# Moving a softmax product and a weight cast of the first batch to GpSimd, and giving its first kv group a bank of its own

## The chip, the cores and the metric

The kernel runs on one core of one Trainium2 chip. The metric is the device time of one execution in microseconds (us); each comparison alternates both kernels on the same chip. A trace covers the span from the first to the last instruction, which is some 1.8 us shorter than the time.

## The reference

Eight batches of attention with separate softmaxes on q and k, then a two-layer network with a swish.

```python
q_s = softmax(q, over head_dim)            # q, k, v: (8, 8, 576, 64), fp32
k_s = softmax(k, over the sequence)
kv  = einsum('bhsd,bhse->bhde', k_s, v)
x   = einsum('bhsd,bhde->bhse', q_s, kv)   # regrouped to (4608, 512)
h   = x @ w_in                             # 512 x 2048
out = (h * sigmoid(beta * h)) @ w_out      # 2048 x 512
```

## The kernel before

The schedule is written by hand: each engine executes its instructions in the order of the program. Batch 0 alone starts with nothing in the chip, so its loads, exponentials, transposes, kv products and weight casts stand in a row. "Pair" is two of the eight heads; `V`, `A`, `G` are VectorE, ScalarE, GpSimd. The helpers that the change touches:

```python
def q_mul(b, s, n=2, eng=nc.vector):       # divides the exponentials by their sums; two SBUF inputs
    eng.tensor_tensor(eq[b][:, :, h, :], eq[b][:, :, h, :],
                      rq[b][:, 1, :, h].unsqueeze(3).to_broadcast((P, R, m, D)), ALU.mult)
def tpe(b, j, tag): ...                    # TensorE transposes pair j into the bank `tag`
def q_ev(b, j, eng): ...                   # copies that bank to SBUF
def vz_cast(b, j, eng, ...): ...           # casts v to bf16 for the kv group j
def kvz_mm(b, j, tag, n): ...              # TensorE: kv of pair j; kvz_norm divides it on VectorE
def xpe(c, j, tag): ...                    # TensorE: x of pair j; xev evicts it
def w_castk(blk, kt, eng): ...             # casts one 128x512 slice of w_in
def hpe(c, j, kts, tag): ...               # TensorE: h[j] += w_in slices kts @ x
def warm(n, tag): ...                      # n dummy matmuls that keep TensorE busy
```

The head of batch 0 (cut; `...` marks cuts):

```python
    q_sum(0, 1, 4)
    q_mul(0, 2, 4)
    kz_exp(0, 0)
    q_mul(0, 1, 4)
    ...
    tpe(0, 3, "acc1")
    tpe(0, 2, "acc3")
    ...
    q_ev(0, 2, V)
    vz_cast(0, 0, G)
    tpe(0, 1, "acc2")
    kvz_mm(0, 0, "acc3", 1)      # waits for the eviction of pair 2 from acc3
    ...
    q_ev(0, 1, V); q_ev(0, 3, V)
    ...
    hpe(0, 2, [3]); hpe(0, 4, [0], "b3") ...   # h of batch 0; blocks j = 4..7 need w_in block 1
```

The softmax here doesn't subtract the row's maximum and nothing guards it: scores larger than these inputs give would overflow.

Of the kernel before, what the change touches and what calls it, by code (L numbers as in the profile page):

```python
# [17 lines left out]
def kernel(  # L18
# [151 lines left out]
    def evac(eng, dst, src):  # L170
        if eng is nc.scalar:
            eng.copy(dst, src)  # L172
        else:
            eng.tensor_copy(dst, src)  # L174
# [8 lines left out]
    def kz_exp(b, j):  # L183
        if j == 0:
            ek_buf(b)
        nc.scalar.activation(ek[b][:, j, :], k_st[b][:, j, :], ACTF.Exp)  # L186
# [28 lines left out]
    def vz_cast(b, j, eng, m=1, part=None):  # L215
        r = slice(0, RW) if part is None else (slice(0, 5), slice(5, RW))[part]
        evac(
            eng,
            va[b][:, j : j + m, r, 0:D],
            v_st[b][:, j : j + m, :].rearrange("p j (i d) -> p j i d", i=RW)[:, :, r, :],  # L220
        )
# [35 lines left out]
    def q_sum(b, s, n=2):  # L257
        if s == 0:
            rq[b] = work.tile([P, 2, R, H], F32, tag="rq", bufs=2, name=f"rq{b}")
        m = H // n  # L260
        h = slice(s * m, (s + 1) * m)
        nc.vector.tensor_reduce(rq[b][:, 0, :, h], eq[b][:, :, h, :], axis=AX.X, op=ALU.add)  # L262
        nc.vector.reciprocal(rq[b][:, 1, :, h], rq[b][:, 0, :, h])  # L263

    def q_mul(b, s, n=2, eng=nc.vector):
        m = H // n
        h = slice(s * m, (s + 1) * m)
        eng.tensor_tensor(  # L268
            eq[b][:, :, h, :],
            eq[b][:, :, h, :],  # L270
            rq[b][:, 1, :, h].unsqueeze(3).to_broadcast((P, R, m, D)),
            ALU.mult,
        )
# [11 lines left out]
    def bank(tag):  # L285
        if tag not in turns:
            return tag
        turns[tag] += 1
        return (HB if tag == "h" else AB)[(turns[tag] - 1) % 2]
# [3 lines left out]
    def tpe(b, j, tag):  # L293
        if j == 0:
            qsT[b] = work.tile([P, R, HP, P], BF16, tag="qsT", bufs=2, name=f"qsT{b}")
        tp_of[b, j] = ps.tile([P, R, P], BF16, tag=bank(tag), bufs=1, name=f"tp{b}_{j}")
        for i in range(R):
            nc.tensor.transpose(  # L298
                tp_of[b, j][:, i, :],
                eq[b][:].rearrange("p i (j x) d -> p i j (x d)", j=HP)[:, i, j, :],  # L300
                identity[:],
            )

    def q_ev(b, j, eng):
        evac(eng, qsT[b][:, :, j, :], tp_of.pop((b, j))[:])

    def kvz_mm(b, j, tag=None, n=1):
        if tag is not None:
            t = ps.tile([P, n, D1], F32, tag=bank(tag), bufs=1, name=f"kv{b}_{j}")
            for jl in range(n):  # L310
                att_of[b, j + jl] = t[:, jl : jl + 1, :]
            att_of[b, j, n] = t
        t = att_of[b, j]
        for i in range(RW):
            for e in range(2):
                r = slice(e * D, (e + 1) * D)
                nc.tensor.matmul(  # L317
                    t[r, 0, :],
                    ek[b][r, j, ds(i * D, D)],
                    va[b][r, j, i, :],  # L320
                    start=(i == 0),
                    stop=(i == RW - 1),
                    tile_position=(e * D, e * D),
                )
# [62 lines left out]
    def xpe(c, j, tag):  # L387
        t = x_ps[c, j] = ps.tile([P, MAIN], F32, tag=bank(tag), bufs=1, name=f"x{c}_{j}")
        nc.tensor.matmul(t[:], kvp[:, c, j, :], qsT[c][:, :, j, :])  # L389

    def xev(c, j, eng, part=None):
        n = MAIN // 2
        cols = slice(0, MAIN) if part is None else slice(part * n, part * n + n)
        evac(eng, x_of(c)[:, j, cols], x_ps[c, j][:, cols])
# [4 lines left out]
    def hpe(c, j, kts, tag="h"):  # L399
        if (c, j) not in h_of:  # L400
            h_of[c, j] = ps.tile([P, MAIN], F32, tag=bank(tag), bufs=1, name=f"h{c}_{j}")
        h = h_of[c, j]
        for kt in kts:
            nc.tensor.matmul(  # L404
                h[:],
                w_unit(j, kt),
                x_of(c)[:, kt, :],
                start=(kt == 0),
                stop=(kt == KT - 1),
            )  # L410
# [117 lines left out]
    def warm(n, tag):  # L528
        t = ps.tile([P, 512], F32, tag=bank(tag), bufs=1, name=f"warm{warm_n[0]}")
        warm_n[0] += 1  # L530
        for _ in range(n):
            nc.tensor.matmul(t[:], xT[2][:, 0, 0:P], xT[2][:, 0, :])  # L532

    V, A, G = nc.vector, nc.scalar, nc.gpsimd
# [22 lines left out]
    def w_castk(blk, kt, eng):  # L557
        evac(eng, w_in_b[blk][kt][:, 0, :], wst["in", blk][:, kt, :])
# [3 lines left out]
    def beta_pe(tag):  # L562
        tb = ps.tile([P, 512], F32, tag=bank(tag), bufs=1, name="tb")
        tb_of.append(tb)
        nc.tensor.transpose(tb[:, 0 : NJ // 2], beta_r[:, 0 : 2 * P : 2], ident8[:])
        nc.tensor.transpose(tb[:, NJ // 2 : NJ], beta_r[:, 1 : 2 * P : 2], ident8[:])

    def beta_ev():
        tb = tb_of[0]
        nc.scalar.copy(  # L570
            beta_t[:].rearrange("p (hh e) -> p e hh", e=2),
            tb[:, 0:NJ].rearrange("p (e hh) -> p e hh", e=2),
        )
# [56 lines left out]
    q_sum(0, 2, 4)  # L630
    q_ev(0, 0, A)
    q_sum(0, 1, 4)
    q_mul(0, 2, 4)
    kz_exp(0, 0)
    q_mul(0, 1, 4)
    warm(10, tag="acc2")
    beta_pe("acc0")
    tpe(0, 3, "acc1")
    tpe(0, 2, "acc3")
    kz_exp(0, 1)  # L640
    beta_ev()
    q_ev(0, 2, V)
    vz_cast(0, 0, G)
    tpe(0, 1, "acc2")
    kz_exp(0, 2)
    kvz_mm(0, 0, "acc3", 1)
    vz_cast(0, 1, G)
    q_ev(0, 1, V)
    q_ev(0, 3, V)
    kz_exp(0, 3)  # L650
    kvz_norm(0, 0)
    kvz_mm(0, 1, "b1", 1)
# [15 lines left out]
    hpe(0, 0, [0], "b0")  # L668
    hpe(0, 1, [0], "b1")
    xev(0, 2, V)  # L670
    w_castk(0, 1, A)
    xpe(0, 3, "acc2")
    w_castk(0, 2, G)
    hpe(0, 3, [0], "b2")
    xev(0, 3, V)
# [314 lines left out]
```

## Time and profile before

| | kernel before |
|---|---|
| time, median of the first three runs | 282.23 us (281.97 to 282.54) |
| span of the profiled run | 279.8 us, clock 1.000 |
| busy share of TensorE / VectorE / ScalarE / GpSimd | 98% / 62% / 58% / 14% |
| idle time in front of TensorE's weight load at 19.4 us | 0.58 us, of which some 0.3 us is a wait for a w_in cast (see the experiments) |

The time view of the page cuts the span in 40 slices of 7 us; each digit is a busy share in tenths.

```profile
PE   8899999999999999999999999999999999999995
DMA  7999999999972993199319941641144034005004
```

TensorE is nearly full throughout, and for the first 11 slices the DMA engines are nearly full as well. So the first 80 us have two candidates for a bound, and which of them wins has to be read wait by wait. The two instructions by which the head will be compared are the first kv matmuls and the last x product (start, length, engine, line, what, count):

```profile
11.10 1.49 PE L317 MATMUL kv<-va,ek 64*64 64x65 bf16 x54
...
14.46 0.39 PE L389 MATMUL x<-qsT,kvp 128*128 128x512 bf16 x1
```

Behind the second one the h matmuls run until they need the later half of w_in block 1.

### The profile page before, as it was taken

What the parts mean: (1) busy time and instruction counts of PE and PEld (TensorE: products, weight loads), DVE (VectorE), ACT (ScalarE), POOL (GpSimd) and SP (SyncE); (2) the same over time, 40 slices, a digit from 0 to 9 for tenths busy, and PEclk for the clock granted to TensorE, in tenths of its full rate; (3) what the DMA queues carried; (4) which work ended last, traced back from release to release, by engine and by line L of the source; (5) the groups of instructions that cost most, each with busy time, mean ns of one, the idle gap of its engine ahead of it and who ended that gap; (6) DMA issues with size and microseconds to landing.
All of it is one profiled execution on the core that took longest, in us unless ns stands there. A gap on an engine that the chain in (4) does not pass through costs nothing.

```text
span 279.8 us, 4474 instructions
## 1 busy us (share of the span) xinstructions
PE 274.7 (98%) x1738; PEld 128.2 (46%) x1738; DVE 174.9 (62%) x285; ACT 162.6 (58%) x248; POOL 39.0 (14%) x59
## 2 busy tenths in 40 slices
PE   8899999999999999999999999999999999999995
PEld 3544454444444444444444444444444544445444
DVE  3964786994478456944595549553864596354362
ACT  3767885947486447744684458444733574454451
POOL 1554237133030003000300030000000000000000
DMA  7999999999972993199319941641144034005004
GB/s 250 389 395 392 386 388 318 331 289 227 270 237 38 253 274 93 64 251 291 96 76 197 305 139 75 134 93 81 69 90 138 0 150 77 0 0 152 0 0 150
DMA packets 55317, 50.09 MB, mean 179 GB/s; under 512 B 26617, under 2 KB 47489, under 8 KB 55297
## 3 DMA queue, kind: packets, MB, share of 16 engines
q1 hardware_dynamic: 54368, 48.97, 59.8%
q10 hardware_dynamic: 928, 0.85, 0.9%
q8 instruction: 13, 0.21, 0.3%
q14 instruction: 8, 0.06, 0.1%
HBM read 36.71 MB, written 9.44 MB: 165 GB/s over the span
## 4 chain that ended last, share of the span: by engine, by line
PE 92%; DMA 6%; SPq 1%; ACT 0%; issue 0%
PE acc L453 44%; PE h L404 43%; DMA w_in<-in_moe_w_in_dram 3%; DMA v_st<-in_v_dram 3%; PE kv L342 2%; PE x L373 1%; PE acc L445 1%; PE kv L317 1%; PE tp L298 0%; PE x L389 0%; ACT w_in_b L172 0%; SPq L578 0%; SPq L132 0%; SPq L109 0%; SPq L135 0%
## 5 line engine op out<-in xcount | busy, mean ns | idle before, releaser
L418 DVE SCALAR_TENSOR_TENSOR g<-th,h 128x512 bf16<-128x512 bf16 x144 | 96.1, 681 | 79.7 <-ACT th L414 79.3
L414 ACT ACTIVATE th<-h,beta_t 128x512 bf16<-128x512 f32 x144 | 97.8, 687 | 81.1 <-PE h L404 80.3
L404 PE MATMUL h<-xT,w_in_b 128*128 128x512 bf16 x576 | 143.3, 379 | 0.1
L453 PE MATMUL acc<-w_out_b,g 128*128 128x512 bf16 x560 | 141.0, 379 | 0.0
L404 PEld LDWEIGHTS <-w_in_b 128*128 128x128 bf16 x576 | 56.0, 98 | 66.4 <-ACT w_in_b L172 0.6
L453 PEld LDWEIGHTS <-g 128*128 128x128 bf16 x560 | 53.8, 98 | 65.9 <-issue 2.5
L174 POOL CAST va<-v_st 128x320 bf16<-128x320 f32 (+2 forms) x14 | 16.6, 1193 | 107.9 <-DMA v_st<-in_v_dram 107.9
L262 DVE TENSOR_REDUCE rq<-eq 128x16 f32<-128x1024 bf16 (+1 forms) x20 | 22.1, 1105 | 5.7 <-ACT eq L251 5.3
L268 DVE TENSOR_TENSOR eq<-eq,rq 128x1024 bf16<-128x1024 bf16 (+1 forms) x19 | 22.1, 1168 | 0.1
L172 ACT CAST xT<-x 128x512 bf16<-128x512 f32 x18 | 9.9, 588 | 16.9 <-PE x L373 14.9
L251 ACT ACTIVATE eq<-q_st 128x1024 bf16<-128x1024 f32 (+1 forms) x18 | 16.9, 955 | 3.5 <-DMA q_st<-in_q_dram 3.5
L174 DVE COPY o<-acc 128x512 f32<-128x512 f32 (+2 forms) x20 | 12.6, 642 | 3.6 <-PE acc L453 3.4
L172 ACT COPY o<-acc 128x512 f32<-128x512 f32 (+1 forms) x18 | 9.5, 571 | 8.6 <-PE acc L453 4.7
L174 DVE CAST xT<-x 128x512 bf16<-128x512 f32 x18 | 11.5, 684 | 2.6 <-PE x L373 1.8
L193 ACT ACTIVATE ek<-k_st 128x1024 bf16<-128x1024 f32 x12 | 12.6, 1051 | 0.0
L532 PE MATMUL warm<-xT 128*128 128x512 bf16 x24 | 7.7, 490 | 1.2 <-DVE xT L613 1.2
L174 POOL CAST w_in_b<-w_in 128x512 bf16<-128x512 f32 (+1 forms) x9 | 5.9, 663 | 6.2 <-DMA w_in<-in_moe_w_in_dram 6.1
L174 POOL CAST w_out_b<-w_out 128x1024 bf16<-128x1024 f32 x5 | 5.2, 1042 | 6.4 <-DMA w_out<-in_moe_w_out_dram 6.4
L186 ACT ACTIVATE ek<-k_st 128x576 bf16<-128x576 f32 x8 | 5.2, 679 | 0.9 <-DMA k_st<-in_k_dram 0.9
L263 DVE RECIPROCAL rq<-rq 128x16 f32<-128x16 f32 (+1 forms) x20 | 4.9, 243 | 0.7
L342 PEld LDWEIGHTS <-ek 128*64 128x64 bf16 x192 | 4.1, 111 | 2.5 <-issue 2.5
L532 PEld LDWEIGHTS <-xT 128*128 128x128 bf16 x24 | 2.8, 121 | 5.2 <-issue 3.0
(49 smaller groups left out, 84.9 us busy)
## 6 DMA issues: line engine op xcount, KB each, us to landing
out_dram<-o SPq DMA_DIRECT2D x14, 512.0 KB, 3.2
q_st<-in_q_dram SPq DMA_DIRECT2D x25, 256.0 KB, 4.1
k_st<-in_k_dram SPq DMA_DIRECT2D x6, 1024.0 KB, 8.7
v_st<-in_v_dram SPq DMA_DIRECT2D x6, 1024.0 KB, 11.3
w_in<-in_moe_w_in_dram SPq DMA_DIRECT2D x6, 512.0 KB, 9.8
v_st<-in_v_dram SPq DMA_DIRECT2D x8, 288.0 KB, 8.0
w_out<-in_moe_w_out_dram SPq DMA_DIRECT2D x4, 512.0 KB, 8.9
w_out<-in_moe_w_out_dram SPq DMA_DIRECT2D x2, 1024.0 KB, 10.4
```

Of the source, the lines that this page charges most:

```text
L172: eng.copy(dst, src)
L174: eng.tensor_copy(dst, src)
L193: nc.scalar.activation(ek[b][:, :, h, :].rearrange("p i h d -> p h i d"), k_st[b][:, h, 0 : R * D].rearrange("p h (i d) -> p h i d", i=R), ...
L251: nc.scalar.activation(eq[b][:, :, s * m : (s + 1) * m, :].rearrange("p i h d -> p h i d"), q_st[b][:, s * m : (s + 1) * m, :].rearrange(" ...
L262: nc.vector.tensor_reduce(rq[b][:, 0, :, h], eq[b][:, :, h, :], axis=AX.X, op=ALU.add)
L268: eng.tensor_tensor(eq[b][:, :, h, :], eq[b][:, :, h, :], rq[b][:, 1, :, h].unsqueeze(3).to_broadcast((P, R, m, D)), ALU.mult,)
L342: nc.tensor.matmul(t[r * D : (r + 1) * D, j, :], ek[b][:, i, hd, :] if i < R else ekt[(b // 2) % 2][:, ds(hd * D, D)], va[b][:, i, hd, :] ...
L404: nc.tensor.matmul(h[:], w_unit(j, kt), x_of(c)[:, kt, :], start=(kt == 0), stop=(kt == KT - 1),)
L414: nc.scalar.activation(th[:], h_of[c, j][:], ACTF.Tanh, scale=beta_t[:, j : j + 1])
L418: nc.vector.scalar_tensor_tensor(out=g[:], in0=th_of.pop((c, j))[:], scalar=1.0, in1=h_of[c, j][:], op0=ALU.add, op1=ALU.mult)
L453: nc.tensor.matmul(acc[st][:], g[:, ds(st * P, P)], w_out_b[:, j, :], start=(j == 0), stop=(j == NJ - 1),)
L532: nc.tensor.matmul(t[:], xT[2][:, 0, 0:P], xT[2][:, 0, :])
```

## The change

It is meant to shorten the head: one product leaves VectorE, pairs 1 and 3 are evicted before pair 2, the first kv group no longer waits for a bank, a dummy fills TensorE's gap, and one weight cast leaves ScalarE.

```diff
-    q_mul(0, 2, 4)
+    q_mul(0, 2, 4, eng=G)
@@
     tpe(0, 3, "acc1")
+    tpe(0, 1, "acc2")
+    q_ev(0, 3, V)
     tpe(0, 2, "acc3")
@@
     beta_ev()
+    q_ev(0, 1, V)
     q_ev(0, 2, V)
     vz_cast(0, 0, G)
-    tpe(0, 1, "acc2")
+    warm(1, tag="b0")
     kz_exp(0, 2)
-    kvz_mm(0, 0, "acc3", 1)
+    kvz_mm(0, 0, "b3", 1)
     vz_cast(0, 1, G)
-    q_ev(0, 1, V)
-    q_ev(0, 3, V)
@@
-    w_castk(0, 1, A)
     xpe(0, 3, "acc2")
+    w_castk(0, 1, G)
     w_castk(0, 2, G)
```

## The prediction

> **What bounds the kernel now.** I read the chain of work that ended last first, because it says which stage a change at the start would have to shorten. These are its pieces around the end of the head (start in us, length in us, what):
>
> ```profile
> 2.68 8.01 DMA v_st<-in_v_dram
> 10.71 8.02 DMA w_in<-in_moe_w_in_dram
> 18.73 0.02 issue
> 18.75 0.63 ACT w_in_b L172
> 19.38 0.05 issue
> 19.43 2.33 PE h L404 x10
> 21.76 3.45 PE acc L453 x16
> ```
>
> The reader is to see that up to 18.73 us the chain holds no batch-0 work at all: only two transfers back to back, the second being the later half of the second w_in block. Then comes one cast on ScalarE, and from 19.43 us on TensorE.
>
> Second, the weight loads of TensorE around that point, with ScalarE's cast (start, length, engine, line, instruction, count, in brackets the idle time before and its releaser):
>
> ```profile
> 18.74 0.10 PEld L404 LDWEIGHTS <-w_in_b 128*128 128x128 bf16 x1 [0.28 <-issue]
> 18.75 0.62 ACT L172 CAST w_in_b<-w_in 128x512 bf16<-128x512 f32 x1 [0.23 <-DMA w_in<-in_moe_w_in_dram]
> 19.42 0.55 PEld L404 LDWEIGHTS <-w_in_b 128*128 128x128 bf16 x4 [0.58 <-ACT w_in_b L172]
> ```
>
> TensorE stands and waits for that slice. How long: the h stream begins to run without gaps behind the last x product, whose load waited for VectorE at 14.46; its first matmul then starts at 14.69. By the program, 20 h matmuls lie between this point and the first that needs the slice. The 28 matmuls of the later row that starts at 25.21 in the chain's unwindowed view take 6.04 us, so 0.216 us each; 14.69 + 20 x 0.216 = 19.01. The next one starts at 19.43. So the head of batch 0 has about **0.4 us of slack** against the transfer: whatever it gains is added to this wait, and it can lose 0.4 us unseen.
>
> Third, the stretches of the head (length, then busy time of PE, PEld, DVE, ACT, POOL with instruction counts, granted clock, DMA share, GB/s):
>
> ```profile
> 10.00:15.00 5.00, 4.40 (x88) 2.69 (x89) 4.58 (x17) 4.08 (x9) 3.79 (x7) 1.00 1.05 384
> 15.00:19.40 4.40, 4.33 (x20) 1.67 (x18) 2.61 (x5) 2.49 (x5) 2.36 (x4) 1.00 1.04 401
> 19.40:35.00 15.60, 15.57 (x73) 7.09 (x74) 9.40 (x15) 12.68 (x19) 6.44 (x7) 1.00 1.05 389
> ```
>
> The transfers are at their rate (384 to 401 GB/s, DMA engines full), so the landing at 18.73 is set by bytes in front of it. SyncE's own waits name only other transfers before this load's issue, no compute. After 19.40 TensorE is busy 15.57 of 15.60 us.
>
> **What the Trainium skill says.** "SBUF — State Buffer", section "Who interferes with whom": a VectorE instruction with two SBUF inputs contends with a GpSimd instruction that reads SBUF; the pair of ports is an exclusive lock for a whole instruction, and issue order decides who blocks. Both q products have two SBUF inputs. The trace agrees, in both orders. GpSimd second (the first v cast, beside two products on VectorE):
>
> ```profile
> 9.28 1.24 DVE L268 TENSOR_TENSOR eq<-eq,rq 128x512 bf16<-128x512 bf16 x2
> 10.00 1.04 POOL L174 CAST va<-v_st 128x576 bf16<-128x576 f32 x1 [1.01 <-DMA v_st<-in_v_dram]
> 10.99 0.67 POOL L174 CAST va<-v_st 128x576 bf16<-128x576 f32 x1
> ```
>
> The same cast takes 1.04 us, then 0.67: it waited until the product was over at 10.52 (9.28 + 1.24). VectorE second, at 55 us:
>
> ```profile
> 54.57 1.93 POOL L174 CAST va<-v_st 128x2048 bf16<-128x2048 f32 x1 [6.94 <-DMA v_st<-in_v_dram]
> 55.63 1.94 DVE L268 TENSOR_TENSOR eq<-eq,rq 128x1024 bf16<-128x1024 bf16 x1
> 56.43 1.61 POOL L233 CAST vt<-v_st 64x512 bf16<-64x512 f32 x1
> 58.68 1.21 DVE L268 TENSOR_TENSOR eq<-eq,rq 128x1024 bf16<-128x1024 bf16 x1
> ```
>
> The product takes 1.94 instead of 1.21 us, so it worked from 56.36 (55.63 + 0.73), just before GpSimd's first cast ends at 56.50; and GpSimd's next cast then took 1.61 us (0.61 where alone). So the engine that waits gets the lock before the other's next instruction.
>
> "GPSIMD Engine Reference", section "Engine selection": elementwise work with two inputs is about twice as slow there as on VectorE. Here a half-size product takes 1.05 us on GpSimd (7.94, one record) against 0.64 to 0.69 on VectorE: 1.6 times.
>
> "TensorE: Matmul & The Clock Gate", section "What's actually happening": the array's clock is halved after an idle window of some 3.4 us and restored after a busy one. The trace shows 14 opening dummies in 5.42 us (0.387 each) and the next 10 in 2.32 (0.232). No idle stretch near 3.4 us exists in the head, nor does the change make one.
>
> **The change part by part.**
> (1) The third product leaves VectorE: minus 0.62 us (1.24 / 2) in its queue, plus 1.05 us on GpSimd. GpSimd does the product before it from 7.94 to 8.99; the sums of the third pair are ready at 8.57 (reciprocal at 8.37, 0.20 long), so the new product runs from 8.99 to about 10.04. VectorE comes to its last product at 9.28, but now GpSimd holds the lock: by the 55 us case it works from about 10.04 - 0.14 = 9.90 and ends at 9.90 + 0.64 = 10.54. Before, that same product ended at 10.52. **The 0.62 us saved comes back as a lock wait of 0.62 us.** The first v cast again queues behind it and ends at 10.54 + 0.52 = 11.06, against 11.04.
> (2) The order of the transposes and evictions: pair 1 can be transposed at about 10.6 as before (10.58), pair 2 right behind it, until about 11.05. VectorE evicts pair 3 from 10.54 and pairs 1 and 2 behind it, three times 0.42 us: to about 11.8 (11.77 before).
> (3) The own bank takes the first kv group's wait for an eviction away. That eviction ended at 10.91 (10.49 + 0.42) and the cast at 11.04, so the wait removed was not the last to end. The dummy adds 0.22 us after the transposes: 11.05 + 0.22 gives a first kv matmul at about 11.3, against 11.10. The first reciprocal of the norms goes from 11.69 to about 11.9. The four norms are a solid VectorE block of 2.75 us (11.69 to 14.44), so the last x product goes from 14.46 to about 14.66 and the slack of 0.4 shrinks to 0.2 us.
> (4) The second w_in slice on GpSimd: 0.61 us there instead of 0.62 on ScalarE (14.15 to 14.77). Its first reader is the third matmul of the h stream, at 14.69 + 2 x 0.216 = 15.12, already late enough before. ScalarE has nothing else to do with the freed time: its next instruction, a th, started at 16.68 after 1.91 us of waiting for TensorE. On GpSimd the slice lands about 13.6 (an estimate, midway between the casts at 12.92 and 14.29 that waited for their slices), and 13.6 + 0.61 = 14.21 fits before 14.29. Nothing moves.
> Sum at the end of the kernel: head +0.2 us, inside the 0.4 us that TensorE waits anyway: **0.0 us**. I write 282.3 for 282.23, the 0.07 for the chance of the second rival.
>
> **The rivals.**
> R1, the author's hope: no lock wait. Then the last product ends at 9.92, the cast at about 10.7, and the norms start perhaps 0.4 us earlier. For it: the engines do become less loaded in the 10 to 15 us stretch, where VectorE is busy 4.58 of 5.00 us. Against it: the 55 us row. It would still end in the same w_in wait, of 0.8 instead of 0.4 us: 282.2. Even if a head gain went through whole, 0.4 us is 0.15%.
> R2, the lock goes badly: GpSimd's v cast takes it once more before VectorE's product gets it. The product then ends at about 11.3, all norms move by some 0.7 to 0.9 us, and 0.3 to 0.5 us come out behind the slack: 282.6 to 282.7. For it: cast and product ask within 0.1 us of each other. Against it: at 56.4 us the waiting product went first.
> R3, the array's clock is halved for one window of 3.4 us by a differently placed gap: half of that, an estimate from the page named, 1.7 us: 284. Against it: gaps under 1 us and a dummy that fills one. I give 2%.
> R4, the landing at 18.73 moves. It hangs on the bytes queued before it, which the change doesn't touch; a later load reuses the first w_in buffer and is issued at 15.59, when its fourth cast is over. That cast should stay where it is.
>
> **Range and chances.** The three runs before span 281.97 to 282.54. My own case and R1 are both within 0.1 us of 282.2, R2 adds up to 0.5; with the scatter of runs the range is 281.7 to 282.9. A gain of 2% is 5.6 us, far more than the whole head could yield; a loss of 2% would need R3 more than thrice. Same: 0.98, 0.01 for each other.
>
> **What would show each step.** Right: the last VectorE product shows about 1.25 us instead of 0.64, GpSimd's second product about 1.05; the first kv matmul at 11.1 to 11.4; the wait of TensorE for the w_in cast still there, about 0.2 us; the chain still through that transfer to 18.7; h from 19.4. Wrong in mechanism: a product of 0.64 us at 9.3 beside GpSimd's (no lock), or a wait that grew to 0.7 (head faster). Wrong in result: no wait at 19.4 any more and later h's shifted (R2), or matmuls of 0.43 us spacing in the head (R3).

## The result

The changed kernel took 281.64 us (median of 6 runs, 281.60 to 282.06), the kernel before 282.1 us in its now six runs (281.58 to 282.54). A ratio is the mean time of one kernel's runs over that of the other's of the same rounds, so not quite the ratio of the medians. Here it is 0.9986 (0.9973 to 0.9999): the same at 2%, though the interval just misses 1. Both profiled spans are 279.8 us. The page after, in the time view:

```profile
PE   8899999999999999999999999999999999999995
DMA  7999999999972991199318961641154034005004
```

The stages that the prediction showed of before, now after (length, then busy time and instruction count of PE, PEld, DVE, ACT, POOL, then clock, DMA share, GB/s):

```profile
10.00:15.00 5.00, 4.09 (x87) 2.54 (x89) 4.36 (x17) 3.46 (x8) 4.40 (x8) 1.00 1.05 387
15.00:19.40 4.40, 4.34 (x20) 1.75 (x18) 2.72 (x5) 2.50 (x5) 2.24 (x4) 1.00 1.03 396
19.40:35.00 15.60, 15.55 (x73) 7.10 (x74) 9.48 (x16) 12.65 (x19) 6.43 (x7) 1.00 1.05 389
```

Between 10 and 15 us ScalarE lost its cast (4.08 to 3.46 us) and GpSimd gained it (3.79 to 4.40); TensorE's work behind 19.40 is unchanged. What became of the product shows in the timeline of VectorE and GpSimd:

```profile
9.28 1.14 DVE L268 TENSOR_TENSOR eq<-eq,rq 128x512 bf16<-128x512 bf16 x1
...
7.82 1.05 POOL L268 TENSOR_TENSOR eq<-eq,rq 128x512 bf16<-128x512 bf16 x1 [5.86 <-ACT eq L251]
8.82 1.05 POOL L268 TENSOR_TENSOR eq<-eq,rq 128x512 bf16<-128x512 bf16 x1
9.87 1.07 POOL L174 CAST va<-v_st 128x576 bf16<-128x576 f32 x1
10.89 0.67 POOL L174 CAST va<-v_st 128x576 bf16<-128x576 f32 x1
```

VectorE's one remaining product takes 1.14 us in place of two times 0.62, GpSimd's second product is over at 9.87, and the v cast behind it takes 1.07 us, where the next, equal one takes 0.67. The two marks of the head:

```profile
11.32 1.16 PE L317 MATMUL kv<-va,ek 64*64 64x65 bf16 x54
...
14.63 0.39 PE L389 MATMUL x<-qsT,kvp 128*128 128x512 bf16 x1
```

Both come later than before. And TensorE's weight loads at the end of the head, with ScalarE's cast:

```profile
18.91 0.10 PEld L404 LDWEIGHTS <-w_in_b 128*128 128x128 bf16 x1 [0.28 <-issue]
19.41 0.11 PEld L404 LDWEIGHTS <-w_in_b 128*128 128x128 bf16 x2 [0.41 <-ACT w_in_b L172]
...
18.74 0.62 ACT L172 CAST w_in_b<-w_in 128x512 bf16<-128x512 f32 x1
```

The load that needs the late slice stands at 19.41, as before (19.42), but only after 0.41 us idle instead of 0.58. The head came 0.17 us later, and the idle time became 0.17 us shorter. Not all of what is left is a wait: 0.25 us stand there even where nothing is waited for, as the experiments show.

The chain of work that ended last, however, no longer goes through the transfer:

```profile
14.76 0.26 PE x L389
15.02 0.05 issue
15.07 3.83 PE h L404 x17
18.90 0.00 issue
18.91 2.85 PE h L404 x12
21.75 3.45 PE acc L453 x16
```

Taken at its word it says that the head is on the path after the change. The experiments have to decide between this and the load rows.

### The profile page after: what moved, and what is told of

It reads as the page before. It is cut to its first block, busy times and chain, and to the rows that moved or that the text cites. A ratio compares the mean times of both kernels' runs of the same rounds, so it can differ in the third digit from the quotient of the medians. Undisturbed runs are those within 1.5% of the kernel's fastest.

```text
span 279.8 us, 4448 instructions
## 1 busy us (share of the span) xinstructions
PE 272.2 (97%) x1712; PEld 128.0 (46%) x1739; DVE 174.9 (63%) x284; ACT 162.0 (58%) x247; POOL 40.5 (14%) x61
## 4 chain that ended last, share of the span: by engine, by line
PE 94%; DMA 3%; issue 1%; DVE 1%; ACT 1%; SPq 0%
PE h L404 45%; PE acc L453 43%; DMA k_st<-in_k_dram 3%; PE kv L342 2%; PE x L373 1%; PE acc L445 1%; PE kv L317 1%; PE x L389 1%; PE tp L298 1%; DVE kvp L332 0%; ACT ek L186 0%; DVE rk L329 0%; SPq L109 0%; ACT o L172 0%; PE x L364 0%
## 5 line engine op out<-in xcount | busy, mean ns | idle before, releaser
L453 PE MATMUL acc<-w_out_b,g 128*128 128x512 bf16 x543 | 137.8, 379 | 1.5 <-issue 1.3
L174 POOL CAST w_in_b<-w_in 128x512 bf16<-128x512 f32 (+1 forms) x10 | 6.5, 656 | 5.7 <-DMA w_in<-in_moe_w_in_dram 5.5
```

Of the source, the lines that this page charges most:

```text
L174: eng.tensor_copy(dst, src)
L453: nc.tensor.matmul(acc[st][:], g[:, ds(st * P, P)], w_out_b[:, j, :], start=(j == 0), stop=(j == NJ - 1),)
```

## The experiments

Twelve kernels ran. T1: what the head does is hidden behind landings (ends) of transfers, and the change is worth nothing. T2: the 0.14% is real.

### Both kernels once more

No edit in either. For `after_again`:

> The changed kernel once more, in more rounds. Theory T1 (whatever the head of batch 0 does is hidden behind the landing of the second w_in block, so the change is worth nothing and the 0.14% of the first result is scatter): ratio to the kernel before 0.999 to 1.001, its interval holding 1. Rival T2 (a small gain that is real): ratio 0.9985 again, about -0.4 us, with an interval clear of 1. In the trace both: VectorE's last product about 1.14 us, TensorE's wait for the w_in cast about 0.25 us.

For `before_again`:

> The kernel before against itself: shows the scatter of the comparison. Both theories: ratio 1.000; if it comes out at 0.9985 or 1.0015, a difference of 0.4 us means nothing here. Its trace: TensorE's wait for the w_in cast again 0.4 us, the weight load row 0.58 us idle.

The changed kernel: 281.74 us, ratio 0.9997 (0.9984 to 1.0011). The kernel before against itself: 281.87 us, ratio 1.000 (0.9987 to 1.0013). The 0.14% did not come again, so the first result looks like scatter; T2 is not excluded, as the new interval still just holds 0.9986. The traces further down show a head that got longer, so nothing is left that a gain could come from. `before_again` also settles how to read the chain. It is the kernel before, only another execution, and its chain goes through the head too:

```profile
14.89 4.42 PE h L404 x19
19.34 2.33 PE h L404 x10
```

In the first execution the same place was a transfer and a cast. A wait of a few tenths of a us is about as long as one matmul record (0.38 us, with a modelled end), and the chain changes its story there without anything having changed.

### The late slices taken away

Both kernels with this edit; the result is wrong.

```diff
     def w_castk(blk, kt, eng):
-        evac(eng, w_in_b[blk][kt][:, 0, :], wst["in", blk][:, kt, :])
+        ks = kt - 2 if blk == 1 and kt >= 2 else kt
+        evac(eng, w_in_b[blk][kt][:, 0, :], wst["in", blk][:, ks, :])
```

On the kernel before:

> Wrong result on purpose: the third and fourth slices of the second w_in block are cast from the staged first and second ones, which land some 2.3 us earlier, so the head of batch 0 meets no late landing. T1: the wait of 0.4 us before the 21st h matmul goes, h runs on from 19.0 us, and all of it arrives at the end: 0.3 to 0.4 us shorter than the kernel before. Rival (the wait is only one of several and the next transfer, w_out or the third w_in block, takes its place): 0.0 to 0.1 us shorter, with a new wait of TensorE after 21 us.

On the changed kernel:

> The same on the changed kernel; wrong result on purpose. With the landing out of the way the change must show what it does to the head. T1 with the working of the prediction: the last x product comes 0.17 us later than in the kernel before, so this one ends 0.1 to 0.2 us later than the same edit on the kernel before, and 0.2 to 0.25 us earlier than the kernel before itself. T2 (the head did gain): it ends 0.2 us or more before the same edit on the kernel before.

Measured: 281.88 us, ratio 1.0002 (0.9988 to 1.0015), and 281.65 us, ratio 1.000 (0.9985 to 1.0015); spans 279.7 and 279.8 us. My expectation failed: no time came out. The trace of the first tells where the gain went. The first w_out matmuls start at 21.30 us instead of 21.60 (0.18 us of which is this execution's earlier start, see the table further down), but at 39 us TensorE's loads and GpSimd read:

```profile
39.10 0.10 PEld L317 LDWEIGHTS <-ek 64*64 64x64 bf16 x1 [0.42 <-ACT va L172]
39.38 0.36 PEld L317 LDWEIGHTS <-ek 64*64 64x64 bf16 x17 [0.18 <-issue]
...
38.57 0.76 POOL L174 CAST va<-v_st 128x320 bf16<-128x320 f32 x1 [2.33 <-DMA v_st<-in_v_dram]
```

The first load is ready at 39.10, the matmuls wait for the cast that ends at 39.33 (38.57 + 0.76), of a v pair that landed at 38.5. So there is a second place where TensorE has almost no slack, which my prediction had not seen. The rival of this expectation, that another wait takes the place of the first, was right, though some 18 us later than it said.

The landing at 38.5 alone does not make this second wait. The same cast takes 0.46 us where it comes first, as in `dummies_6` further down; here it stands beside a product of VectorE (the first line is this run's, the other two are from `dummies_6`):

```profile
37.81 1.21 DVE L268 TENSOR_TENSOR eq<-eq,rq 128x1024 bf16<-128x1024 bf16 x1
...
38.76 0.46 POOL L174 CAST va<-v_st 128x320 bf16<-128x320 f32 x1 [2.57 <-DMA v_st<-in_v_dram]
38.87 1.42 DVE L268 TENSOR_TENSOR eq<-eq,rq 128x1024 bf16<-128x1024 bf16 x1
```

The cast ends 0.31 us after the product (39.02 to 39.33), and in `dummies_6`, where the cast came first, the product is the longer one. By an estimate from these, 38.57 + 0.46 = 39.03, the cast would have been over before TensorE's load at 39.10 but for this lock on SBUF reads. No run takes the lock away and leaves the landing. Another 0.17 us of the gain had gone before: the first w_out matmul starts at 21.30, in `nowait2_before` (next section) at 21.13 with its last x product at the same time. It is a stop of TensorE for which the trace names no releaser.

### Both landings taken away

The same edit and, in `vz_cast`, the first v pair of batch 1 read from one that landed earlier (wrong again):

```diff
+        js = 2 if b == 1 and j == 0 else j
-            v_st[b][:, j : j + m, :].rearrange(...)
+            v_st[b][:, js : js + m, :].rearrange(...)
```

On the kernel before:

> Wrong result on purpose. The last run on the kernel before, without the late w_in slices, moved h up by some 0.3 us at 21 us, and lost it at 39.1 us, where TensorE waited for the cast of the first v pair of batch 1 (landed at 38.5). Here that cast reads a pair that landed earlier as well. Theory T1b (two landings, w_in at 18.7 and v at 38.5, each pin the end): both waits gone, the profiled span 0.2 to 0.4 us under that of the kernel before (279.4 to 279.6), kv of batch 1 at about 39.0 without a wait. Rival: something further down, as the next v pair at 40.7, takes it again and the span stays at 279.7 to 279.8.

On the changed kernel:

> The same on the changed kernel, wrong result on purpose. T1b: what the change does to the head shows at last: its h stream starts 0.15 to 0.35 us later than that of the same edit on the kernel before, and so do the first w_out matmuls and the end; profiled span 279.6 to 279.8. If the change helped the head, its span would be under the other's.

Measured spans of the profiled runs: **279.3 us and 279.7 us**. Timed: 281.51 us, ratio 0.9992 (0.9970 to 1.0014), and 281.47 us, ratio 0.9984 (0.9968 to 1.0000); these don't tell the two apart (the two fastest of six runs are 281.03 and 281.09 us, against 281.40 twice), so the verdict rests on the traces, one each. The last x product and the h stream behind it, in the kernel before with this edit,

```profile
14.27 0.39 PE L390 MATMUL x<-qsT,kvp 128*128 128x512 bf16 x1
14.50 6.80 PE L405 MATMUL h<-xT,w_in_b 128*128 128x512 bf16 x30
```

and in the changed kernel with this edit:

```profile
14.65 0.39 PE L390 MATMUL x<-qsT,kvp 128*128 128x512 bf16 x1
14.88 6.80 PE L405 MATMUL h<-xT,w_in_b 128*128 128x512 bf16 x30
```

Thirty h matmuls take 6.80 us in each, with the stop of 0.17 us at the 19th (in the kernel before the 19th starts at 18.74, 0.38 us after the 18th, where 0.216 is usual) but no wait for a cast, and the 0.38 us between the two streams arrive at the end as 0.4 us of span. Some 0.09 us of it is this execution's own start (GpSimd's first product begins at 7.84 against 7.75), the rest the change. With the landings out of the way the changed kernel is the slower one.

How much the first wait hides can now be read without the chain. In these two runs TensorE needs 6.86 and 6.87 us from the last x product to the first w_out matmul (14.27 to 21.13; 14.65 to 21.52). In the two traces of the kernel before it took 7.14 and 7.05 us, in the two of the changed kernel 6.96 and 6.91 us. So the wait for the w_in cast was 0.2 to 0.3 us before and 0.05 to 0.1 us after the change: the head was nearly on the path, and the chain of `after` was not far wrong. Behind the first kv matmul of batch 1, at about 39 us, nothing differs: in all 14 traces the span ends 240.3 to 240.4 us after it.

### The slack measured from the other side

```diff
-    warm(1, tag="b0")
+    warm(6, tag="b0")
```

> The changed kernel with six dummies in place of one before the first kv group: the head 5 x 0.216 = 1.08 us later, result right. T1: 0.25 us of it goes into the wait that is left there for the w_in cast, the rest, 0.8 us, arrives at the end (ratio 1.003 to the kernel before, span 280.5 to 280.7), and no wait for a w_in cast is left. If it is hidden elsewhere (more slack than I read): ratio 1.000.

282.65 us, ratio 1.0022 (1.0007 to 1.0037), span 280.6 us. The last x product came 0.99 us later than in the first trace of the changed kernel (15.62 against 14.63), and the span grew by 0.8: about 0.2 us had been slack, not the 0.25 us at the w_in cast alone that I expected. About 0.1 us of it was there (6.96 against 6.86 us, see above), the rest at the second wait, which is gone here. The load of the late slice still stands idle 0.25 us, but that is no wait: the same row in `nowait2_before` has 0.25 too, and its matmuls go on 0.216 us apart.

```profile
20.24 0.83 PEld L404 LDWEIGHTS <-w_in_b 128*128 128x128 bf16 x5 [0.25 <-ACT w_in_b L172]
```

### The lock

GpSimd works as long, but reads nothing from SBUF:

```diff
-    q_mul(0, 2, 4, eng=G)
+    G.memset(eq[0][:, :, 4:6, :], 0.0625)
+    G.memset(eq[0][:, :, 4:6, :], 0.015625)
```

> Wrong result on purpose: GpSimd's second product is replaced by two memsets of the same tile, 0.53 us each by the memset of as many elements at 46.6 us, so GpSimd is as long at work but reads nothing from SBUF. If VectorE's last product waited for the lock that GpSimd's reads hold, it now takes 0.64 us in place of 1.14 and ends at about 9.85, pair 1 is transposed some 0.5 us earlier; if it was slow for another reason, it stays at 1.14. The time: unchanged, since the head that gains 0.3 to 0.5 us only waits longer for the w_in cast (0.5 to 0.7 us in place of 0.25): ratio 0.999 to 1.001.

```profile
9.23 0.69 DVE L268 TENSOR_TENSOR eq<-eq,rq 128x512 bf16<-128x512 bf16 x1
...
8.77 0.53 POOL L633 MEMSET eq<- 128x512 bf16 x1
9.35 0.53 POOL L634 MEMSET eq<- 128x512 bf16 x1
```

VectorE's product falls from 1.14 to 0.69 us, at the same hour and beside a GpSimd that is just as busy. So it was the lock on reads. The last x product comes at 14.13, half a us earlier than in the changed kernel, and the time is 281.81 us, ratio 0.9994 (0.9975 to 1.0013): this head gain buys nothing either. (The result still passed the comparison, as the constant is near the true values.)

The wait for the w_in cast was 1.05 us here (idle time of the matmuls; 1.54 us in the load row) and not the 0.5 to 0.7 that I expected, and the profiled span 280.5 us. The chain of this execution says why:

```profile
10.68 8.68 DMA w_in<-in_moe_w_in_dram
19.36 0.02 issue
19.38 0.63 ACT w_in_b L172
20.01 0.04 issue
20.05 2.33 PE h L404 x10
```

The slice landed at 19.36, not 18.73, 0.63 us later than in the first execution of the kernel before; the span is 0.7 us longer, although the head was early. That is what a bound by a landing looks like, and one cause of the runs' scatter. Whether the other long runs have the same cause is open: they left no trace, and some of them (two of 282.50 us, one of 283.04) show a granted clock of 0.994 in place of 0.998 to 1.000, which is another candidate.

### One part undone at a time

Three looks, each the changed kernel with one edit. The product back on VectorE:

```diff
-    q_mul(0, 2, 4, eng=G)
+    q_mul(0, 2, 4)
```

> The changed kernel with the third product back on VectorE, all else as changed. If the move's saving is all paid back as a lock wait, VectorE's two products show 0.62 us each in a row from about 9.2 and end at about 10.4, where the single one ended before (10.42), and the first kv matmul stays at 11.2 to 11.35. If the move had gained something, kv comes later by up to 0.6 us. Time: one run, 281.5 to 282.8 as all.

The dummy left out:

```diff
-    warm(1, tag="b0")
```

> The changed kernel without the dummy in front of the first kv group. Working of the prediction: the dummy holds the first kv group back by 0.2 us; without it kv starts at about 11.1 and the last x product about 0.2 us earlier (14.4 to 14.5 in place of 14.6), and TensorE's wait for the w_in cast is 0.4 again. Rival: the v cast or the norm chain is the last to end and nothing moves. No change of the matmuls' spacing (clock) in either.

The cast back on ScalarE:

```diff
+    w_castk(0, 1, A)
     xpe(0, 3, "acc2")
-    w_castk(0, 1, G)
```

> The changed kernel with the second w_in slice back on ScalarE. Expected: that cast at about 14.3 to 14.9 us on ScalarE, h stream without a gap at its third matmul or one under 0.1 us, all else in place; the move of this cast is worth nothing.

Times: 281.52, 281.52 and 281.62 us, one run each. Each execution's q data lands up to 0.2 us apart, so I count from the start of GpSimd's first product to the start of the last x product, both from the timelines:

| kernel | first product, us | last x product, us | head, us |
|---|---|---|---|
| before; before_again; nowait_before; nowait2_before; two_splits | 7.94; 7.93; 7.76; 7.75; 7.83 | 14.46; 14.45; 14.28; 14.27; 14.36 | 6.52 to 6.53 |
| after; after_again; nowait_after; nowait2_after | 7.82; 7.72; 7.84; 7.84 | 14.63; 14.52; 14.65; 14.65 | 6.80 to 6.81 |
| product_back | 7.73 | 14.52 | 6.79 |
| no_dummy | 7.88 | 14.51 | 6.63 |
| cast_back | 7.91 | 14.72 | 6.81 |
| memset_for_product | 7.78 | 14.13 | 6.35 |
| dummies_6 | 7.73 | 15.62 | 7.89 |

Counted like this the traces repeat within 0.01 us, and the head got **0.29 us longer**. The dummy is 0.18 of it, the product 0.02, the cast 0.00; the remaining 0.09 belongs to the new order and bank, by subtraction, not by a run of its own. The traces show where it sits: the first transpose behind the last product starts 0.06 us after that product's end in the old order (10.52 to 10.58 in `before`), 0.15 us in the new one (10.42 to 10.57 in `after`, and as much in `no_dummy`). Why is not shown. The two products of `product_back` stand in one row,

```profile
9.07 1.24 DVE L268 TENSOR_TENSOR eq<-eq,rq 128x512 bf16<-128x512 bf16 x2
```

and end at 10.31 (9.07 + 1.24), 2.58 us after the first product; in the changed kernel the single one ends at 10.42, 2.60 us after it. The 0.62 us saved are wholly paid back.

### An attempt at a faster kernel

On the kernel before, result right:

```diff
     def w_castk(blk, kt, eng):
-        evac(eng, w_in_b[blk][kt][:, 0, :], wst["in", blk][:, kt, :])
+        m = 2 if blk == 1 and kt >= 2 else 1
+        for i in range(m):
+            c = ds(i * 512 // m, 512 // m)
+            evac(eng, w_in_b[blk][kt][:, 0, c], wst["in", blk][:, kt, c])
@@
-    q_mul(1, 1)
+    q_mul(1, 2, 4)
+    q_mul(1, 3, 4)
```

> An attempt to beat both, on the kernel before, result right: the casts of the two late w_in slices in two halves each, so the h matmul that waits needs only the first half (0.39 in place of 0.62 us), and VectorE's product of the second half of batch 1 in two, so GpSimd's cast of the first v pair, landed at 38.5, waits for a shorter lock. Theory: TensorE goes on some 0.2 us earlier at 19.2, and at 39.1 in place of 39.4: span 279.5 to 279.7 against 279.8, ratio 0.999. Rival: dependences are kept by whole tile or bank, or the landings' scatter swallows it: ratio 1.000.

281.88 us, ratio 1.0014 (0.9993 to 1.0034), span 279.7 us: not faster. The first split works, the second doesn't (loads of TensorE, its first kv matmuls of batch 1, GpSimd's cast, VectorE's halves):

```profile
19.23 1.84 PEld L404 LDWEIGHTS <-w_in_b 128*128 128x128 bf16 x10 [0.50 <-ACT w_in_b L172]
...
39.36 0.47 PE L317 MATMUL kv<-va,ek 64*64 64x65 bf16 x18
...
38.45 0.86 POOL L174 CAST va<-v_st 128x320 bf16<-128x320 f32 x1 [2.23 <-DMA v_st<-in_v_dram]
...
37.71 1.28 DVE L268 TENSOR_TENSOR eq<-eq,rq 128x512 bf16<-128x512 bf16 x2
```

TensorE goes on at 19.23, 0.46 us after ScalarE's cast began at 18.77, where before it was 0.67 (18.75 to 19.42). But at 38.45 the second half of the product was already at work, so the cast waited for it and ended at 39.31; the kv matmuls stand at 39.36, against 39.40 in `before_again`. A gain at the first wait is lost at the second, as in `nowait_before`.

## Why the prediction was right

"Same" held. The time did so only roughly: 282.3 was said and 281.64 measured, 0.06 us under the lower end of the stated range (281.7). The working started from the first three runs of the kernel before (282.23); later rounds of that kernel gave medians of 281.69 to 281.93. By its steps:

- **The bound.** Held in kind: a head 0.17 us shorter than before (memsets, 6.35 against 6.52) or 0.29 us longer (the change) leaves the time, and about 1 us on top of that comes through as 0.8. Its size did not hold. The slack was 0.2 to 0.3 us and not 0.4, since the sum of 20 matmuls at 0.216 us has no term for the stop of 0.17 us at the 19th. The picture was also incomplete: there are two waits in a row, for w_in at 18.7 and for the v cast at 39.3, and even without the first nothing is gained.
- **The product (1).** Held. A lock wait was to eat the saving; the product ended at 10.42 (10.54 said), with 1.14 us (1.25 said). GpSimd's first product began 0.12 us earlier than in the profile I had worked from, and all that hangs on it did too.
- **Order and evictions (2).** Nothing was to move. By subtraction 0.09 us did.
- **Bank and dummy (3).** Kv at 11.3 and the last x product at 14.66 were said; 11.32 and 14.63 came. Against their own start, though, it is +0.29, not +0.2: the term for the order was missing, and that 14.63 still met 14.66 is luck, as the start was 0.12 us early. The remaining slack was 0.05 to 0.1 us, not 0.2. A loss a little larger would have shown, as `dummies_6` does.
- **The cast (4).** Worth 0.00, as said; its place in the gap on GpSimd fitted (13.49 to 14.10).
- **R1** (no lock wait) was produced on purpose by the memsets, and ended the same, as said. **R2** did not occur: GpSimd's cast, asking at 9.87, let VectorE's waiting product go first. **R3** did not occur: h matmuls keep 0.216 us spacing in the head.
- **One sign was wrong.** I said the chain would still go through the transfer. It didn't, in the changed kernel nor in the second execution of the kernel before; it is not fit to tell waits of 0.3 us and less.

## What to carry to other kernels

Before shortening a stage, look for the transfers that land after it: here heads of 6.35 to 6.81 us give the same time within the scatter, because TensorE waits for a landing at 18.7 us and again for a cast at 39.3 us. Work moved to GpSimd to relieve VectorE saved nothing here, since VectorE's next product has two SBUF inputs and waited while GpSimd read. And count a stage from its own first instruction: then traces repeat within 0.01 us, where whole times scatter by 0.3%.

## What the Trainium skill lacked or had wrong

- "SBUF — State Buffer", section "Who interferes with whom", says who blocks whom, and the runs agree: 1.14 us beside a GpSimd product, 0.69 beside memsets, which only write. It lacks who comes next when both wait: here a waiting VectorE product went ahead of GpSimd's next cast (that cast took 1.07 us, the following one 0.67), and likewise at 55 us in the kernel before (1.61 us instead of 0.61).
- "GPSIMD Engine Reference", section "Engine selection", gives about 2 to 1 for elementwise work with two inputs. The 128x512 product here took 1.05 us against 0.64 to 0.69 us, so 1.5 to 1.6 to 1; its inputs are bf16 and broadcast fp32.
- No page that I found has the scatter of a landing from execution to execution: the same w_in slice, behind the same loads, landed at 18.73 and at 19.36 us, and spans of 279.8 and 280.5 us followed it.
